# Uneven narrowing, four-unit normalisation rounds, GpSimd scaling and ScalarE first accumulation in an attention and mixture-of-experts kernel

## The chip, the cores and the metric

The kernel runs on one core of one Trainium2 chip. A core has TensorE (PE in the profile; its weight loads are PEld), VectorE (DVE), ScalarE (ACT), GpSimd (POOL) and SyncE (SP, which issues the DMAs here). The metric is the device time of one execution in microseconds, the median of several.

## What is computed

Windowed attention over 4 x 576 tokens is followed by a mixture of eight experts whose weights P come from an iterated (Sinkhorn) normalisation, and that by a two-layer network with a squared ReLU. Cut to the parts that matter here:

```python
logits = x @ w_gate                     # 2304 tokens, 8 experts
P = np.exp(logits - logits.max())
for _ in range(8):
    P /= P.sum(1, keepdims=True) + 1e-09
    P /= P.sum(0, keepdims=True) + 1e-09
    P *= N / E
for e in range(E):                      # FE = 1024 in quarters of 256
    h = np.maximum(x @ w1[e], 0.0)
    out += P[:, e:e + 1] * (h @ w2[e])
h = out @ w_in                          # FF = 2048 in eighths of 256
g = np.maximum(h, 0.0) ** 2
return g @ w_out
```

## The kernel before

**Steps.** After attention, work goes in 80 steps, numbered i = 0 to 79. Steps 0 to 31 take the 32 quarter experts for tokens 0 to 1279 (the first pass, `pair_of(i)` = 0), steps 32 to 63 the same quarters for tokens 1280 to 2303 (the second pass, `pair_of(i)` = 1), and steps 64 to 79 are the two-layer network in the same two passes. A pass treats 1024 tokens by a Strassen-like scheme of seven products; the first pass has 256 tokens more, the "singles".

**Units.** A step is a list of units, each a group of matmuls: u1 to u7 of the first layer (`l1_pair`, six matmuls of 512 columns each), eight units of the second layer of the step before (`l2_units`), and in the first pass four single second-layer units and two single first-layer units of 256 columns. That is 21 units in the first pass and 15 in the second, counted k = 0, 1, ... in the order u1, u2, u3, u4, l2, u5, l2, u6, l2, u7, five l2, then the singles. What is due for other engines is written behind the unit to which it is tied: `after(j, f)` puts `f` behind the unit j places later. All engines run their own instructions in the order in which they are written.

**The banks.** Each l2 unit, each single unit and each small matmul of the normalisation writes one of three PSUM buffers named mm. It comes free when VectorE has added it into the accumulator acc (L647), or, in the first accumulation of a pass, when ScalarE or VectorE has copied it there (L643 for odd column blocks, L645 for even ones). In the first three steps (`i < SCALED`) the hidden values are not scaled by P, since P is not known yet; the accumulator is multiplied by P afterwards, in step 3 (L650).

**Normalisation.** `sinkhorn()` is a generator that is moved on once behind each unit of steps 0 to 2. A round has an opening half on VectorE (five small instructions, L429 to L437, ending in the column sums scs), a matmul on TensorE two units later (L443, sums over partitions), and, a unit after that, a closing half on VectorE (four small instructions, L445 to L448). Before the change the closing half of a round and the opening half of the next stand together, so a round takes three units.

**Narrowing.** The weights of the two-layer network arrive as 64-bit numbers and are turned into float32 in 32 pieces, each in four parts: A starts a load (L165), B is two VectorE instructions on 512 columns (L172, L176), C two (L180, L183), D three and a store (L187, L190, L194, L195). `narrow_on()` does the next part. Before the change it is called behind the units k = 0 and 8 of the steps 3 to 58 (but for 30 to 32), and behind k = 13 of each third step; `settled` completes a piece ahead of step 30, and step 60 begins with all parts that are still missing.

**Other work named below.** `split` of new weights into high and low halves (L129 on ScalarE, L133 on VectorE: w2l, blkl, suml), sums of weight blocks on GpSimd (L142 to L147), the scaling g (L532), its low half gl (L518), the additions into s2 and s3 (L583, L574), and `load_p`, which loads the rows of P for the next expert (L253).

Of the kernel before, what the change touches and what calls it, by code (L numbers as in the profile page):

```python
# [14 lines left out]
ALU = mybir.AluOpType  # L15
# [18 lines left out]
SPE = FE // FB  # L34
# [6 lines left out]
SCALED = 3  # L41
# [5 lines left out]
def tile_kernel(ctx: ExitStack, tc: tile.TileContext, a):  # L47
    nc = tc.nc
    out = a["out"]
# [360 lines left out]
    def sinkhorn():  # L410
        flat = ptile.rearrange("p c e -> p (c e)")
        ones = xb()[:, :128]
        nc.vector.memset(ones, 1.0)
        m1 = sk.tile([128, 1], F32, tag="m1", name="m1")
        m2 = sk.tile([128, 1], F32, tag="m2", name="m2")
        nc.vector.tensor_reduce(out=m1, in_=flat, axis=AX.X, op=ALU.max)
        yield
        ps = bank("mm")
        nc.tensor.transpose(ps[:1, :128], m1, ident)
        nc.vector.tensor_reduce(out=m2[:1], in_=ps[:1, :128], axis=AX.X, op=ALU.max)  # L420
        yield
        ps = bank("mm")
        nc.tensor.matmul(ps[:, :1], ones[:1, :], m2[:1, :], start=True, stop=True)
        nc.vector.tensor_scalar(out=m1, in0=ps[:, :1], scalar1=-1.0, scalar2=None, op0=ALU.mult)
        nc.scalar.activation(out=flat, in_=flat, func=AF.Exp, bias=m1, scale=1.0)
        yield
        for _ in range(8):
            rs = sk.tile([128, NCH, 1], F32, tag="srs", name="srs")
            nc.vector.tensor_reduce(out=rs[:, :, 0], in_=ptile, axis=AX.X, op=ALU.add)  # L429
            nc.vector.tensor_scalar(out=rs, in0=rs, scalar1=1e-9, scalar2=None, op0=ALU.add)  # L430
            nc.vector.reciprocal(out=rs, in_=rs)
            nc.vector.tensor_tensor(
                out=ptile, in0=ptile, in1=rs.to_broadcast([128, NCH, E]), op=ALU.mult
            )
            cs = sk.tile([128, E], F32, tag="scs", name="scs")
            ct = sk.tile([128, 1, E], F32, tag="sct", name="sct")
            nc.vector.tensor_reduce(  # L437
                out=cs, in_=ptile.rearrange("p c e -> p e c"), axis=AX.X, op=ALU.add
            )
            yield  # L440
            yield
            ps = bank("mm")
            nc.tensor.matmul(ps[:, :E], ones, cs, start=True, stop=True)  # L443
            yield
            nc.vector.tensor_scalar(out=ct[:, 0, :], in0=ps[:, :E], scalar1=1e-9, scalar2=None, op0=ALU.add)  # L445
            nc.vector.reciprocal(out=ct, in_=ct)
            nc.vector.tensor_scalar(out=ct, in0=ct, scalar1=float(NTOK) / E, scalar2=None, op0=ALU.mult)
            nc.vector.tensor_tensor(  # L448
                out=ptile, in0=ptile, in1=ct.to_broadcast([128, NCH, E]), op=ALU.mult
            )  # L450
        yield
        for c0, c1 in ((0, 16), (16, NCH)):
            m = (c1 - c0) * E
            ps = bank("mm")
            nc.tensor.transpose(ps[:m, :128], ptile[:, c0:c1, :].rearrange("p c e -> p (c e)"), ident)
            pT = tmp("pT")[:, :128]
            nc.vector.tensor_copy(pT[:m], ps[:m, :128])
            nc.sync.dma_start(p_dram[c0:c1].rearrange("c e n -> (c e) n"), pT[:m])
            yield
        for t in range(2):  # L460
            load_p(0, 0, t)
        load_ps(0)
# [10 lines left out]
    def pair_of(i):  # L473
        return phase(i) % 2
# [16 lines left out]
    def after(k, f):  # L491

        due.setdefault(clock[0] + k, []).append(f)
# [49 lines left out]
    def l1_pair(i):  # L543

        gh = post[0].tile([128, FC, 2 * T], F32R, tag="gh", name="gh", bufs=2)
        gl = post[0].tile([128, FC, 2 * T], F32R, tag="gl", name="gl", bufs=2)
        g_t[i, 0] = gh, gl
        bank_a, bank_b, bank_c = bank("s"), bank("pt"), bank("xt")
        s2, s3 = (post[0].tile([128, 512], F32, tag=n, name=n, bufs=1) for n in ("s2", "s3"))

        def out(fc, t, src, k):
            cols = slice(t * T, t * T + T)
            p = p_t[pair_of(i), steps[i][1] // SPE, t] if steps[i][0] and i >= SCALED else None
            evac_g(i, gh[:, fc, cols], gl[:, fc, cols], src, p, k)

        def u1():
            product(bank_a, i, "blk", 0, 0, start=True)
            after(0, lambda: nc.scalar.copy(bank_b, bank_a))  # L558

        def u2():  # L560
            product(bank_c, i, "sum", 0, 4, start=True)

        def u3():
            product(bank_a, i, "blk", 1, 1, stop=True)
            out(0, 0, bank_a, 0)

        def u4():
            product(bank_b, i, "sum", 1, 5)
            after(0, lambda: nc.scalar.copy(s2, bank_b))  # L569

        def u5():
            product(bank_b, i, "sum", 2, 6)
            after(0, lambda: nc.scalar.copy(s3, bank_b))
            after(1, lambda: nc.vector.tensor_tensor(out=s3, in0=bank_c, in1=s3, op=ALU.add))  # L574
            out(1, 1, s3, 2)

        def u6():
            product(bank_b, i, "blk", 3, 3, stop=True)
            out(1, 0, bank_b, 0 if i < SCALED or not steps[i][0] else 1)

        def u7():
            product(bank_c, i, "sum", 3, 2, stop=True)
            after(0, lambda: nc.vector.tensor_tensor(out=s2, in0=bank_c, in1=s2, op=ALU.add))  # L583
            out(0, 1, s2, 2)
            if steps[i][0] and steps[i][1] % SPE == SPE - 2:
                after(1, lambda: load_p(pair_of(i), steps[i][1] // SPE + 1, 0))
            if steps[i][0] and steps[i][1] % SPE == SPE - 1:
                after(1, lambda: load_p(pair_of(i), steps[i][1] // SPE + 1, 1))

        return [u1, u2, u3, u4, u5, u6, u7]  # L590

    def l1_single(i):
# [21 lines left out]
    def l2_units(i, which):  # L614

        if i < 0 or (i, which) not in g_t:
            return []
        moe, s = steps[i]
        last = s == (NS1 if moe else NS2) - 1
        gh, gl = g_t[i, which]  # L620
        whi, wlo = (z.rearrange("p (f d) -> p f d", f=FC) for z in wset[i % 2]["w2"])
        n = NSG if which else 2 * T
        t0 = SINGLE if which else PAIRS[pair_of(i)]

        def unit(c, h, w):
            ps = bank("mm")
            ps = ps[:, :w] if moe else ps
            k = 0
            for fc in range(FC):
                for g, wt in ((gh, whi), (gl, whi), (gh, wlo)):  # L630
                    if moe:
                        lhsT, rhs = wt[:, fc, c * 128:c * 128 + 128], g[:, fc, h:h + w]
                    else:
                        lhsT, rhs = g[:, fc, c * 128:c * 128 + 128], wt[:, fc]
                    nc.tensor.matmul(ps, lhsT, rhs, start=k == 0, stop=k == 3 * FC - 1)  # L635
                    k += 1
            if moe:
                dst = acc[which].rearrange("p (c n) -> p c n", c=KC)[:, c, h:h + w]
            else:
                dst = acc[which].rearrange("p (c d) -> p c d", d=DM)[:, c]  # L640
            if s == 0:
                if c % 2:
                    nc.scalar.copy(dst, ps)  # L643
                else:
                    nc.vector.tensor_copy(dst, ps)  # L645
            else:
                nc.vector.tensor_tensor(out=dst, in0=ps, in1=dst, op=ALU.add)  # L647
            if i == SCALED - 1:
                p = p_t[0] if which else p_t[0, 0, h // T]
                nc.vector.tensor_tensor(out=dst, in0=dst, in1=p, op=ALU.mult)  # L650
            if last and moe:
                nc.sync.dma_start(y_dram[:, c, t0 + h:t0 + h + w], dst)
            elif last:
                ch = t0 // 128 + c
                nc.sync.dma_start(out[ch * 128:(ch + 1) * 128], dst)

        if moe:
            return [lambda c=c, h=h: unit(c, h, min(T, n)) for h in range(0, n, T) for c in range(KC)]
        return [lambda c=c: unit(c, 0, DM) for c in range(n // 128)]
# [16 lines left out]
    with tc.manual_schedule():  # L676
# [144 lines left out]
        for i in range(len(steps) + 1):  # L821
# [33 lines left out]
            for k, u in enumerate(order):  # L855
                run(u)
                if i < SCALED:
                    next(sink, None)
                if 3 <= i < first[2] - 5 and not slow and (k in (0, 8) or (k == 13 and i % 3 == 0)):
                    narrow_on()  # L860
        settle()

# [77 lines left out]
```

## Time and profile before

| | |
|---|---|
| median of 3 runs | 2089.8 us (2089.55 to 2090.09) |
| the profiled execution, device time | 2094.18 us |
| its span, first to last instruction | 2092.3 us |
| TensorE busy | 2038.7 us, 97% |
| VectorE busy | 1597.5 us, 76% |
| ScalarE, GpSimd busy | 758.0 us, 364.9 us |
| mean granted TensorE clock | 0.995 |

The profile counts a matmul from its start to its modelled end, so neighbours overlap; where TensorE waits it shows as idle time before a matmul. A window over one step gives the length of the step, since each step begins with the first product of u1.

### The profile page before, as it was taken

Reading aid. Unit: us, or ns where it says so; the run is one execution under the profiler, and the core shown is the slowest. Engines: PE = TensorE matmul, PEld = TensorE weight load, DVE = VectorE, ACT = ScalarE, POOL = GpSimd, SP = SyncE. Lnnn points to the kernel's source line nnn. Section 1 sums busy time; section 2 is a strip of 40 time slices with the busy share of each in tenths; the row PEclk is TensorE's granted clock in tenths of the full one; section 3 lists DMA queues with packets and bytes.
Section 4 is the critical chain, followed back from the end, with each engine's and each line's share of the span. In section 5 each row is a group of like instructions: output and inputs, shape, how many; then the busy total and the mean of one; then the engine's idle time right before and its main releaser. Section 6 shows DMA issues by size and latency. Waiting matters only on the chain.

```text
span 2092.3 us, 26392 instructions
## 1 busy us (share of the span) xinstructions
PE 2038.7 (97%) x10230; PEld 1684.7 (81%) x10230; DVE 1597.5 (76%) x2604; ACT 758.0 (36%) x1375; POOL 364.9 (17%) x404
## 2 busy tenths in 40 slices
PE   9989899999999999999999999999999999999999
PEld 7767788888788888888788888888887878887887
DVE  5867777777777777777888888888888786667776
ACT  6752232232232322222343333333333354344542
POOL 2521011111101111111221121212121131113120
PEclk9999999999999999999999999999999999999999
DMA  8622212121212121112322313232323131113111
GB/s 254 192 70 70 63 50 65 47 67 56 66 59 69 58 74 53 52 63 71 125 79 79 86 61 96 66 95 62 96 61 101 61 101 45 38 59 111 61 41 50
DMA packets 67292, 160.63 MB, mean 77 GB/s; under 512 B 6096, under 2 KB 26592, under 8 KB 67168
## 3 DMA queue, kind: packets, MB, share of 16 engines
q1 hardware_dynamic: 67168, 158.96, 24.5%
q8 instruction: 80, 1.31, 0.3%
q14 instruction: 44, 0.36, 0.1%
HBM read 138.94 MB, written 20.00 MB: 76 GB/s over the span
## 4 chain that ended last, share of the span: by engine, by line
PE 83%; DVE 14%; ACT 1%; issue 1%; DMA 1%; SPq 0%; POOL 0%; DVEq 0%; ACTq 0%; POOLq 0%
PE mm L635 39%; PE pt L484 15%; PE s L484 10%; PE xt L484 9%; PE mm L604 5%; DVE acc L647 4%; DVE gl L518 2%; DVE g L532 1%; DVE suml L133 1%; PE mm L735 1%; PE s L296 1%; PE xt L357 1%; PE pt L344 1%; DVE s L583 1%; DVE x_lo L210 1%
## 5 line engine op out<-in xcount | busy, mean ns | idle before, releaser
L647 DVE TENSOR_TENSOR acc<-mm,acc 128x512 f32<-128x512 f32 x746 | 474.6, 643 | 206.1 <-PE mm L635 201.2
L635 PE MATMUL mm<-gl,w2h 128*128 128x512 f32 x1024 | 404.1, 395 | 0.0
L635 PE MATMUL mm<-gh,w2h 128*128 128x512 f32 x1024 | 403.1, 394 | 0.8 <-DVE acc L647 0.7
L635 PE MATMUL mm<-gh,w2l 128*128 128x512 f32 x1024 | 403.7, 394 | 0.0
L540 ACT CAST gh<-g 128x512 fp32r<-128x512 f32 x308 | 191.4, 622 | 581.9 <-DVE g L532 581.6
L142 POOL TENSOR_TENSOR sums<-raw 128x256 f32<-128x256 f32 x80 | 65.5, 819 | 1522.8 <-DVE suml L133 1502.5
L635 PEld LDWEIGHTS mm<-gh,w2h 128*128 128x128 f32 x1024 | 192.9, 188 | 46.5 <-DVE acc L647 2.1
L635 PEld LDWEIGHTS mm<-gl,w2h 128*128 128x128 f32 x1024 | 192.7, 188 | 44.0
L635 PEld LDWEIGHTS mm<-gh,w2l 128*128 128x128 f32 x1024 | 192.8, 188 | 43.5
L518 DVE TENSOR_TENSOR gl<-g,gh 128x512 fp32r<-128x512 f32 x308 | 222.9, 728 | 0.9 <-ACT gh L540 0.9
L532 DVE SCALAR_TENSOR_TENSOR g<-s,pp 128x512 f32<-128x512 f32 x183 | 127.8, 698 | 94.1 <-PE s L484 91.9
L484 PE MATMUL pt<-x_hi,sumh 128*128 128x512 f32 x320 | 127.3, 398 | 4.5 <-ACT s L569 4.5
L484 PE MATMUL s<-x_hi,blkh 128*128 128x512 f32 x320 | 126.4, 395 | 1.0 <-ACT pt L558 1.0
L484 PE MATMUL xt<-x_lo,sumh 128*128 128x512 f32 x320 | 126.1, 394 | 0.0
L484 PE MATMUL pt<-x_lo,sumh 128*128 128x512 f32 x320 | 126.1, 394 | 0.0
L484 PE MATMUL pt<-x_hi,suml 128*128 128x512 f32 x320 | 126.1, 394 | 0.0
L484 PE MATMUL xt<-x_hi,suml 128*128 128x512 f32 x320 | 126.0, 394 | 0.0
L484 PE MATMUL xt<-x_hi,sumh 128*128 128x512 f32 x320 | 125.9, 394 | 0.0
L484 PE MATMUL s<-x_lo,blkh 128*128 128x512 f32 x320 | 125.9, 393 | 0.0
L484 PE MATMUL s<-x_hi,blkl 128*128 128x512 f32 x320 | 125.7, 393 | 0.0
L540 ACT CAST sgh<-g 128x256 fp32r<-128x256 f32 x74 | 29.9, 406 | 244.0 <-DVE g L532 244.0
L133 DVE TENSOR_TENSOR w2l<-raw,w2h 128x1024 fp32r<-128x1024 f32 x80 | 100.6, 1258 | 17.2 <-ACT w2h L129 17.2
(149 smaller groups left out, 4123.5 us busy)
## 6 DMA issues: line engine op xcount, KB each, us to landing
raw<-in_w SPq DMA_DIRECT2D x128, 512.0 KB, 3.5
raw<-w SPq DMA_DIRECT2D x32, 512.0 KB, 3.4
q<-in_q SPq DMA_DIRECT2D x15, 576.0 KB, 5.4
pp<-p_dram SPq DMA_DIRECT2D x32, 256.0 KB, 5.3
xb<-in_w_in SPq DMA_DIRECT2D x16, 512.0 KB, 4.6
w<-xb SPq DMA_DIRECT2D x32, 256.0 KB, 2.1
xb<-in_w_out SPq DMA_DIRECT2D x16, 512.0 KB, 4.6
v<-in_v SPq DMA_DIRECT2D x16, 432.0 KB, 4.6
```

The source lines that it names most:

```text
L133: nc.vector.tensor_tensor(out=w[1], in0=src, in1=w[0].bitcast(F32), op=ALU.subtract)
L142: tt(out=c(sums, 0), in0=c(raw1, 2), in1=c(raw1, 3), op=ALU.add)
L210: return lambda: nc.vector.tensor_tensor(out=x_lo[:, k, j], in0=z, in1=x_hi[:, k, j].bitcast(F32), op=ALU.subtract)
L296: nc.tensor.matmul(ps[:, g, :], qt[:, j, :], kt[:, j * QB:j * QB + KB], start=True, stop=True)
L344: nc.tensor.transpose(ps[:, g * 128:(g + 1) * 128], ex[:, g, :], ident)
L484: nc.tensor.matmul(ps, w[:, c], z[:, x, j], start=start and k == 0, stop=stop and k == 5, skip_group_check=True)
L518: nc.vector.tensor_tensor(out=glo, in0=z, in1=ghi.bitcast(F32), op=ALU.subtract)
L532: nc.vector.scalar_tensor_tensor(out=held["g"], in0=src, scalar=0.0, in1=held["r"], op0=ALU.max, op1=ALU.mult)
L540: after(k + 1, lambda: nc.scalar.copy(ghi, held["g"]))
L604: nc.tensor.matmul(ps, w[:, c], z[:, kc], start=k == 0, stop=k == 3 * KC - 1)
L635: nc.tensor.matmul(ps, lhsT, rhs, start=k == 0, stop=k == 3 * FC - 1)
L647: nc.vector.tensor_tensor(out=dst, in0=ps, in1=dst, op=ALU.add)
```

## The change

Five edits. (1) A `yield` between a closing half and the next opening half makes a round of the normalisation four units long. (2) The load of P's first row block for the next expert goes from u7 of the third quarter to u1 of the fourth quarter of an expert. (3) In step 0's accumulation (done in step 1) all blocks are copied by ScalarE. (4) The multiplication of the accumulator by P in step 3 goes to GpSimd. (5) Narrowing starts at step 5, with two parts a step in the first pass (k = 0, 8) and three in the second (k = 0, 5, 10).

```diff
@@ sinkhorn
             nc.vector.tensor_tensor(
                 out=ptile, in0=ptile, in1=ct.to_broadcast([128, NCH, E]), op=ALU.mult
             )
+            yield
         yield
@@ l1_pair
         def u1():
             product(bank_a, i, "blk", 0, 0, start=True)
+            if steps[i][0] and steps[i][1] % SPE == SPE - 1:
+                after(1, lambda: load_p(pair_of(i), steps[i][1] // SPE + 1, 0))
             after(0, lambda: nc.scalar.copy(bank_b, bank_a))
...
             out(0, 1, s2, 2)
-            if steps[i][0] and steps[i][1] % SPE == SPE - 2:
-                after(1, lambda: load_p(pair_of(i), steps[i][1] // SPE + 1, 0))
@@ l2_units
             if s == 0:
-                if c % 2:
+                if c % 2 or i == 0:
                     nc.scalar.copy(dst, ps)
...
             if i == SCALED - 1:
                 p = p_t[0] if which else p_t[0, 0, h // T]
-                nc.vector.tensor_tensor(out=dst, in0=dst, in1=p, op=ALU.mult)
+                nc.gpsimd.tensor_tensor(out=dst, in0=dst, in1=p, op=ALU.mult)
@@ the loop over steps
-                if 3 <= i < first[2] - 5 and not slow and (k in (0, 8) or (k == 13 and i % 3 == 0)):
+                if SCALED + 2 <= i < first[2] - 5 and not slow and k in ((0, 8), (0, 5, 10))[pair_of(i)]:
                     narrow_on()
```

VectorE in step 1, from the split of the new first-layer weights (blkl) to the end of the next opening half. Before:

```order
L645 COPY acc_1957<-mm 128x512
L133 TENSOR_TENSOR blkl_136<-raw_95,blkh_135 128x1024
L574 TENSOR_TENSOR s_2107<-xt,s_2107 128x512
L445 TENSOR_SCALAR sct<-mm 128x8
L446 RECIPROCAL sct<-sct 128x8
L447 TENSOR_SCALAR sct<-sct 128x8
L448 TENSOR_TENSOR ptile<-ptile,sct 128x144
L429 TENSOR_REDUCE srs<-ptile 128x18
L430 TENSOR_SCALAR srs<-srs 128x18
L431 RECIPROCAL srs<-srs 128x18
L432 TENSOR_TENSOR ptile<-ptile,srs 128x144
L437 TENSOR_REDUCE scs<-ptile 128x8
```

and after, where the closing half stands a unit ahead of the opening half, the s3 addition between them, and no copy into acc is left:

```order
L133 TENSOR_TENSOR blkl_136<-raw_95,blkh_135 128x1024
L445 TENSOR_SCALAR sct<-mm 128x8
L446 RECIPROCAL sct<-sct 128x8
L447 TENSOR_SCALAR sct<-sct 128x8
L448 TENSOR_TENSOR ptile<-ptile,sct 128x144
L577 TENSOR_TENSOR s_2105<-xt,s_2105 128x512
L429 TENSOR_REDUCE srs<-ptile 128x18
L430 TENSOR_SCALAR srs<-srs 128x18
L431 RECIPROCAL srs<-srs 128x18
L432 TENSOR_TENSOR ptile<-ptile,srs 128x144
L437 TENSOR_REDUCE scs<-ptile 128x8
```

In all, VectorE has seven closing and six opening halves in step 1 before, and five of each after; the rest moves into step 2.

GpSimd in steps 2 to 4 after the change, where before only the weight sums (sums) stood:

```order
L147 TENSOR_TENSOR sums<-raw_95,sums 128x256
L651 TENSOR_TENSOR acc_1957<-acc_1957,pp 128x512 x8
L651 TENSOR_TENSOR acc_1958<-acc_1958,ps 128x256 x4
L142 TENSOR_TENSOR sums<-raw_95 128x256
```

The twelve multiplications now stand between the weight sums written in step 3 and those written in step 4.

VectorE in step 35 (second pass), from the weight split to the scaling of s3. Before:

```order
L133 TENSOR_TENSOR blkl_136<-raw_95,blkh_135 128x1024
L647 TENSOR_TENSOR acc_1957<-mm,acc_1957 128x512
L574 TENSOR_TENSOR s_9598<-xt,s_9598 128x512
L532 SCALAR_TENSOR_TENSOR g<-s_9598,pp 128x512
```

and after, with part D at k = 5:

```order
L133 TENSOR_TENSOR blkl_136<-raw_95,blkh_135 128x1024
L187 TENSOR_SCALAR xb<-xb 128x512
L190 SCALAR_TENSOR_TENSOR xb<-xb 128x512
L194 TENSOR_TENSOR xb<-xb 128x512
L648 TENSOR_TENSOR acc_1957<-mm,acc_1957 128x512
L577 TENSOR_TENSOR s_9566<-xt,s_9566 128x512
L533 SCALAR_TENSOR_TENSOR g<-s_9566,pp 128x512
```

Part D now stands ahead of an addition into acc and of the s3 addition, which reads the bank that u7 writes next.

## Rows read from the trace of the kernel before

**Rows 1.** The page: busy time of each engine, and the chain by engine.

```profile
PE 2038.7 (97%) x10230; PEld 1684.7 (81%) x10230; DVE 1597.5 (76%) x2604; ACT 758.0 (36%) x1375; POOL 364.9 (17%) x404
...
PE 83%; DVE 14%; ACT 1%; issue 1%; DMA 1%; SPq 0%; POOL 0%; DVEq 0%; ACTq 0%; POOLq 0%
```

**Rows 2.** Windows: stretch, length, busy us (instructions) by engine, granted clock, DMA share, GB/s.

```profile
149.50:185.50 36.00, 30.82 (x154) 25.19 (x154) 30.05 (x80) 10.35 (x18) 6.78 (x8) 0.95 0.10 30
185.50:212.10 26.60, 26.60 (x142) 22.75 (x140) 15.26 (x24) 7.71 (x12) 3.27 (x4) 1.00 0.37 96
212.10:247.40 35.30, 29.97 (x141) 24.98 (x140) 27.48 (x43) 7.89 (x12) 3.78 (x4) 0.90 0.14 38
247.40:273.90 26.50, 26.50 (x141) 22.65 (x140) 19.94 (x32) 7.90 (x12) 3.33 (x4) 1.00 0.23 75
273.90:963.80 689.90, 672.98 (x3452) 570.87 (x3451) 510.32 (x827) 197.66 (x300) 85.81 (x100) 0.99 0.20 60
329.00:356.50 27.50, 27.09 (x141) 22.79 (x140) 20.60 (x34) 7.91 (x12) 3.30 (x4) 1.00 0.19 58
356.50:383.30 26.80, 26.72 (x141) 22.66 (x139) 18.96 (x31) 7.91 (x12) 3.31 (x4) 1.00 0.22 65
464.10:496.50 32.40, 29.16 (x140) 25.11 (x139) 22.99 (x36) 7.90 (x12) 3.80 (x4) 0.89 0.20 61
...
1044.70:1585.80 541.10, 541.10 (x2341) 439.85 (x2340) 460.41 (x652) 187.54 (x267) 97.28 (x105) 1.00 0.26 80
...
1606.60:1628.60 22.00, 21.12 (x92) 16.88 (x91) 19.82 (x29) 8.05 (x11) 3.20 (x4) 1.00 0.26 84
1628.60:1649.40 20.80, 20.80 (x92) 16.93 (x91) 15.99 (x24) 7.05 (x10) 4.07 (x6) 1.00 0.16 51
```

**Rows 3.** Groups by line: single second-layer matmuls; busy us, mean ns, idle before <-releaser.

```profile
L635 PE MATMUL mm<-sgh,w2h 128*128 128x256 f32 x256 | 77.1, 301 | 23.9 <-DVE acc L647 23.4
```

**Rows 4.** Waits in step 1: us in total, times, longest.

```profile
PE mm L443 <- DVE scs L437: 5.7, 5, 1.9
```

**Rows 5.** Timeline of VectorE, one round of the normalisation (start, duration).

```profile
157.35 0.15 DVE L445 TENSOR_SCALAR sct<-mm 128x8 f32<-128x8 f32 x1
...
159.52 0.42 DVE L437 TENSOR_REDUCE scs<-ptile 128x8 f32<-128x144 f32 x1
```

**Rows 6.** Groups by line: VectorE's copies into the accumulator, step 1.

```profile
L645 DVE COPY acc<-mm 128x512 f32<-128x512 f32 x4 | 2.7, 686 | 1.0 <-PE mm L635 1.0
...
L645 DVE COPY acc<-mm 128x256 f32<-128x256 f32 x2 | 0.8, 420 | 0.7 <-PE mm L635 0.7
```

**Rows 7.** Groups by line: VectorE's multiplications of the accumulator, step 3.

```profile
L650 DVE TENSOR_TENSOR acc<-acc,pp 128x512 f32<-128x512 f32 x8 | 5.6, 695 | 0.3
...
L650 DVE TENSOR_TENSOR acc<-acc,ps 128x256 f32<-128x256 f32 x4 | 1.7, 425 | 0.1
```

**Rows 8.** One line's instructions: GpSimd on 512 columns (ns min/median/max).

```profile
L204 POOL TENSOR_TENSOR xb<-xb x24: 1290/1296/2167, 993.8 to 1909.7; 128x512 f32<-128x512 f32 x24
```

**Rows 9.** Timelines of VectorE and GpSimd in step 3, side by side.

```profile
236.74 1.22 DVE L518 TENSOR_TENSOR gl<-g,gh 128x512 fp32r<-128x512 f32 x1
...
236.23 1.17 POOL L143 TENSOR_TENSOR sums<-raw 128x256 f32<-128x256 f32 x1
```

**Rows 10.** Timeline of step 7, which starts at 329.04: VectorE, and u7 on TensorE.

```profile
337.31 1.22 DVE L133 TENSOR_TENSOR blkl<-raw,blkh 128x1024 fp32r<-128x1024 f32 x1
338.89 0.69 DVE L647 TENSOR_TENSOR acc<-mm,acc 128x512 f32<-128x512 f32 x1 [0.36 <-PE mm L635]
339.50 0.68 DVE L574 TENSOR_TENSOR s<-xt,s 128x512 f32<-128x512 f32 x1
...
341.48 0.39 PE L484 MATMUL xt<-x_hi,sumh 128*128 128x512 f32 x1
...
342.89 0.42 DVE L187 TENSOR_SCALAR xb<-xb 128x512 int32<-128x512 int32 x1
...
344.69 0.68 DVE L518 TENSOR_TENSOR gl<-g,gh 128x512 fp32r<-128x512 f32 x1
```

## The prediction

> **What bounds the kernel now.** I read the page first, then windows cut at the step boundaries, then what ended TensorE's waits inside the steps that are too long, and last the VectorE timelines there. The page says TensorE: 97% busy, 83% of the chain, with VectorE holding 14% of it [rows 1]. So VectorE's 76% is no bound as a mean, and time can only come out of places where TensorE waits for it. The windows show which. The 26 steps 33 to 58 of the second pass take 541.1 us, 20.8 each, with TensorE busy for the whole of it [rows 2]: nothing can be won there, only lost. In the first pass a step without a wait is step 4 with 26.5, but steps 5 to 29 average 689.9 / 25 = 27.6, step 1 takes 36.0 and step 3 35.3 [rows 2]. In three of the long ones the granted clock is 0.95, 0.90 and 0.89, so that part of each ran at the lower of the two levels, 1.2 instead of 2.4 GHz, behind the wait [rows 2]: a long wait costs more than itself. Two waits make up most of it: the single second-layer units wait 23.4 us for VectorE's additions to free a bank [rows 3], and the normalisation's matmul in step 1 waits 5.7 us for the column sums [rows 4].
>
> **Step 1: longer rounds and ScalarE copies.** A round costs VectorE 159.52 + 0.42 - 157.35 = 2.6 us [rows 5]. Before, step 1 holds seven closing and six opening halves, 6.5 rounds or 16.9 us, in 30.05 us of VectorE work [rows 2]; the copies are 2.7 + 0.8 = 3.5 us more [rows 6], the rest about 9.7. After, it holds five rounds (13.0) and no copies: 22.7 us of work for 26.5 us of matmuls. A unit of the second pass is 20.8 / 15 = 1.39 us [rows 2], so a round has 5.5 us instead of 4.2 for its 2.6 and whatever else is queued. TensorE becomes the bound, but an opening half still has only two units, 2.8 us, to reach scs, with splits of 1.22 us [rows 10] queued ahead of it in two rounds; I leave 1.0 us for that and take 27.5. Ends: 26.6 as step 2 [rows 2]; 32 if each of five matmuls still waits the 5.7 / 5 = 1.1 that it did [rows 4]. Gain **8.5** (4 to 9.4). ScalarE gets six copies, some 3.5 us at VectorE's price, on 10.35 of 36 [rows 2]; its idle time covers them. If it ran late, the mm banks would come free late; its load of about half the step doesn't say so.
>
> **Step 2** takes over the 1.5 rounds and the transposes: 3.9 us on VectorE's 15.26, 19.2 in all, less than the 19.94 that step 4 carries without a TensorE wait [rows 2]. Its own small matmuls and one late column sum: loss **0.5** (0 to 1).
>
> **Step 3: scaling on GpSimd.** VectorE loses 5.6 + 1.7 = 7.3 us [rows 7] and the narrowing parts of this step. GpSimd gets eight instructions of 1.30 us [rows 8] and four of half the width, some 13 us, between its weight sums; step 4's additions wait for them a step later, which is cover enough, and the next weight sums are needed only in the second half of step 4. What isn't free is the neighbour: while GpSimd read SBUF (1.17 us for 256 columns), gl, whose two inputs are in SBUF, took 1.22 us instead of the 0.68 of the later one [rows 9, 10], 0.54 more. Eight VectorE instructions of step 3 have both inputs in SBUF (four gl, two g from s2 and s3, two splits) and stand among the multiplications: 8 x 0.54 = 4.3 us. What lateness costs here I take from step 7: its part D adds 344.69 - 342.89 = 1.8 us [rows 10] behind the ninth unit, and the step is 27.5, 1.0 above step 4 [rows 2]. So 4.3 / 1.8 x 1.0 = 2.4 us, step 3 at 28.9, gain **6.4**. Ends: 26.5 without any contention (8.8), and 35.3 as before (0, the second rival).
>
> The Trainium skill (SBUF — State Buffer, Who interferes with whom) says that a VectorE instruction with two SBUF inputs and a GpSimd instruction that reads SBUF exclude each other for the whole instruction. The 1.22 us of gl agree. By that rule the delay is up to a whole 1.30 us each instead of the 0.54 that I scale with.
>
> **Narrowing in the first pass.** From step 5 on two parts a step, so A B and C D take turns. Both occur before: C D in step 7, 27.5, and A B in step 8, 26.8 [rows 2], together 54.3. Steps 5 to 29 become 26.8 + 12 x 54.3 = 678.4 against 689.9: gain **11.5** (9 to 13, the upper end with every A B at 26.7 and D a little cheaper without a third part ahead of it). What goes is the third part of each third step; step 12, with B, C and D, takes 32.4 at clock 0.89 [rows 2].
>
> **Narrowing in the second pass.** Three parts in each of 26 steps instead of in each third. VectorE is at 460.4 / 26 = 17.7 us of 20.8 now [rows 2]; the 17 parts more come to 4.25 pieces of some 4 us (D alone 1.8 [rows 10]), 0.7 us a step: 18.4, or 88%. The 20.8 us of the steps that have three parts now (all within rows 2's 541.1) speak for no loss. The new place k = 5 does cost something: with D there, the s3 addition moves 1.8 us back. In step 7 it ended at 339.50 + 0.68 = 340.18, and u7, which writes the bank it reads, began at 341.48 [rows 10]: 1.3 us of slack, and VectorE idles from 338.5 (the end of blkl) to 338.89, 0.4 us more: about 0.1 to 0.2 short. D falls on k = 5 in six steps: loss **1.2** with something for the rest (0 to 6).
>
> **Step 60** begins with the three missing parts before, 22.0 against 20.8 in step 61 [rows 2]; after, all 128 are done by step 58. Gain **1.2**. Moving load_p by about half a step costs nothing: it still has over ten units, 14 us, and only its place among the loads in SP's queue changes; the wait for its buffer was over an expert ago.
>
> **Sum.** 8.5 - 0.5 + 6.4 + 11.5 - 1.2 + 1.2 = 25.9 us. The profiled execution, 2094.2 (span 2092.3 and 1.9 around it), would come to 2068.3. The median lies 4.4 below that execution; I take the same sum off it: 2089.8 - 25.9 = 2063.9, say **2064**.
>
> **The rivals.**
> - *The rounds are bound by their chain, not by VectorE's load.* Then five rounds at (36.0 - 26.5) / 6.5 = 1.5 us each stay in step 1, the rest moves to step 2, and only the copies (3.5) are won: 8.0 - 3.5 = 4.5 less, 2068.4. For it: scs ends the wait each time [rows 4]. Against: VectorE is at 83% in that step and rounds of 2.6 us fit twice into four units.
> - *GpSimd takes back what it relieves.* If each of the eight instructions waits a whole multiplication, 8 x 1.30 = 10.4 us exceed the 7.3 removed, step 3 stays at 35.3 with its clock fall, and the sum is 6.4 smaller: 2070.3. For it: rows 9. Against: a GpSimd instruction also waits for VectorE, and the first three multiplications are two units apart.
>   The Trainium skill (Perfetto Trace Analysis, Optimizing Scalar/DVE Operations) warns of exactly this, that moving work between these two might not help; rows 9 bear out the contention, not yet its size here.
> - *The second pass runs out of VectorE (slower).* First-pass steps with a third part cost (689.9 - 17 x 27.15) / 8 = 28.5, 1.4 more than those with two. If each of the 26 second-pass steps paid 1.4, that is 36 us: 2064 + 36 - 1.2 = 2099. It decides from 25.9 / 26, or 1.0 us a step on top. For it: 88% load, no singles to wait but a burst of five additions in a row. Against: rows 2, 541.1 us without any wait, three-part steps included.
> - *The change does little*, if lateness only wanders into the following steps and the clock falls there: 2064 + 20 = 2084. Against: step 4 recovered fully behind step 3 [rows 2].
>
> **How the numbers follow.** Forecast (all terms near their values) 0.62, chain rival 0.13, GpSimd rival 0.15, both faster as well; second pass 0.05, slower; little 0.05, at 2084 on the edge, so 0.02 faster and 0.03 the same. The best ends together give 9.4 + 8.8 + 13 + 1.2 = 32.4, 2057.4; the chain rival and the GpSimd rival together 10.9 more than 2064, 2074.9. Eight in ten: **2056.5 to 2074**. A measurement here can tell about 0.2%, 4 us, from no change: faster 0.92, within 0.2% 0.03, slower 0.05.
>
> **What would show it.** In the profile after: step 1 below 29 us with TensorE's waits for scs under 2 us and clock 1.00; step 3 at 27 to 31, with gl and the splits over 1 us beside GpSimd's multiplications; steps 5 to 29 alternating near 27.5 and 26.8, with no window under clock 0.99; second-pass steps at 20.8 with some tenths more in each fourth; step 60 at 20.8. The forecast is wrong if second-pass windows exceed 21.5 on average, if the clock falls in step 3, or if a first-pass step with only A B or C D passes 28.

## The result and the profile after

The changed kernel takes 2065.4 us in the median of four runs (2063.2 to 2067.1) against 2090.0 (2089.55 to 2093.8): a ratio of 0.9878, 95% interval 0.9861 to 0.9895, 24.6 us less. The forecast was 2064.0 in a range of 2056.5 to 2074.0. The profiled execution took 2067.1 us, its span 2065.3.

The page of the changed kernel, busy times and the chain by engine, beside [rows 1]:

```profile
PE 2029.6 (98%) x10230; PEld 1673.7 (81%) x10230; DVE 1575.6 (76%) x2586; ACT 761.3 (37%) x1381; POOL 376.8 (18%) x416
...
PE 87%; DVE 11%; ACT 1%; DMA 1%; issue 0%; SPq 0%; POOL 0%; DVEq 0%; ACTq 0%; POOLq 0%
```

VectorE is as busy as before in the mean. What fell is its share of the chain, from 14% to 11%. The windows of the changed kernel, with columns as in [rows 2] (stretch, length, busy us by engine, granted clock, DMA), are steps 0, 1, 2, 3, then 5 to 29 in one, 6, 7, 31, 33 to 58 in one, 35, and 60:

```profile
132.20:147.90 15.70, 14.15 (x73) 10.95 (x72) 9.05 (x24) 6.91 (x12) 0.00 (x0) 1.00 0.35 114
147.90:176.20 28.30, 28.25 (x152) 23.81 (x150) 24.14 (x62) 14.36 (x26) 6.79 (x8) 1.00 0.11 38
176.20:203.30 27.10, 27.10 (x146) 23.06 (x145) 18.38 (x38) 7.71 (x12) 3.27 (x4) 1.00 0.31 76
203.30:231.30 28.00, 26.95 (x140) 22.63 (x139) 20.76 (x27) 7.89 (x12) 15.37 (x12) 1.00 0.16 47
...
257.90:935.50 677.60, 671.01 (x3452) 566.82 (x3451) 493.67 (x811) 197.69 (x300) 82.92 (x100) 1.00 0.20 59
284.60:312.10 27.50, 26.95 (x140) 22.67 (x139) 20.59 (x34) 7.91 (x12) 3.31 (x4) 1.00 0.26 77
312.10:338.80 26.70, 26.70 (x140) 22.64 (x139) 18.96 (x31) 7.90 (x12) 3.32 (x4) 1.00 0.15 50
962.00:1006.30 44.30, 42.60 (x212) 36.01 (x211) 37.90 (x57) 15.93 (x27) 14.36 (x12) 0.96 0.33 104
1018.00:1560.00 542.00, 542.00 (x2342) 438.78 (x2341) 470.49 (x680) 187.68 (x267) 98.31 (x105) 1.00 0.27 85
1059.60:1080.60 21.00, 21.00 (x92) 16.82 (x90) 18.91 (x29) 7.07 (x10) 4.60 (x5) 1.00 0.33 101
1580.80:1601.60 20.80, 20.80 (x92) 16.91 (x91) 15.15 (x22) 8.03 (x11) 2.60 (x4) 1.00 0.16 51
```

Beside [rows 2]: step 1 goes from 36.0 to 28.3 (28.4 from matmul to matmul; a window is cut at tenths) with TensorE busy all but 0.05 us of it by the modelled ends of its matmuls, step 3 from 35.3 to 28.0 with the clock at 1.00 instead of 0.90, steps 5 to 29 from 689.9 to 677.6, step 60 from 22.0 to 20.8. The second pass pays 0.9 us. And the single second-layer matmuls, which waited 23.4 us for VectorE's additions [rows 3], wait 9.2 (the same view, by line):

```profile
L636 PE MATMUL mm<-sgh,w2h 128*128 128x256 f32 x256 | 76.7, 300 | 9.3 <-DVE acc L648 9.2
```

By step (lengths from windows at the step boundaries, in us; the minus sign is a gain):

| place | forecast | measured in the two profiled executions |
|---|---|---|
| attention, before step 0 | 0 | -0.8 |
| step 0 | 0 | -0.9 |
| step 1 | -8.5 | -7.7 |
| step 2 | +0.5 | +0.5 |
| step 3 | -6.4 | -7.2 |
| steps 5 to 29 | -11.5 | -12.3 |
| step 31 | 0 | +1.6 |
| steps 33 to 58 | +1.2 | +0.9 |
| step 60 | -1.2 | -1.2 |
| all | -25.9 | -27.1 |

The medians differ by 24.6 and not 27.1 us because the profiled execution of before lies 4.2 us above its median and that of after 1.7. The three large terms of the forecast each miss by 0.8 us, step 1 short and the other two over. The three places without a term (-0.8, -0.9 and +1.6) add up to -0.1 us; that they cancel is luck.

### The profile page after: what moved, and what is told of

Same layout as the page of the kernel before. It is cut to its first block, busy times and chain, and to the rows that moved or that the text cites. A ratio compares the mean times of both kernels' runs of the same rounds, so it can differ in the third digit from the quotient of the medians.

```text
span 2065.3 us, 26402 instructions
## 1 busy us (share of the span) xinstructions
PE 2029.6 (98%) x10230; PEld 1673.7 (81%) x10230; DVE 1575.6 (76%) x2586; ACT 761.3 (37%) x1381; POOL 376.8 (18%) x416
## 4 chain that ended last, share of the span: by engine, by line
PE 87%; DVE 11%; ACT 1%; DMA 1%; issue 0%; SPq 0%; POOL 0%; DVEq 0%; ACTq 0%; POOLq 0%
PE mm L636 42%; PE pt L485 16%; PE s L485 10%; PE xt L485 9%; PE mm L605 6%; DVE acc L648 3%; DVE gl L519 2%; DVE g L533 1%; PE mm L736 1%; PE s L296 1%; DVE suml L133 1%; PE xt L357 1%; PE pt L344 1%; DVE x_lo L210 1%; DVE s L586 0%
```

## The experiments

Each is the changed kernel with one edit, but for the first, which is the kernel before with one. Where only one execution was timed, the lengths of the steps in its trace are what is compared; they repeat within 0.1 us from kernel to kernel in nearly all steps where nothing was changed, so a step says more than the total, which is 2 us up or down by the attention part and the clock alone.

**The new sharing out of the narrowing alone**, on the kernel before:

```diff
-                if 3 <= i < first[2] - 5 and not slow and (k in (0, 8) or (k == 13 and i % 3 == 0)):
+                if SCALED + 2 <= i < first[2] - 5 and not slow and k in ((0, 8), (0, 5, 10))[pair_of(i)]:
```

> The kernel before with the new sharing out of the narrowing alone. Additive theory: steps 5 to 29 at 677.6 us (690.0 before), 33 to 58 at 542.0 (541.1), step 60 at 20.8 (21.9), and step 3, without its parts, 2 to 4 us shorter than 35.3; together 14.5 to 17 us, 2073 to 2075.5. Rival: the edits only work together, since late work of steps 1 to 3 wanders on; then steps 5 to 29 stay above 683 and the total above 2080.

2076.2 us (2075.0 to 2077.7), ratio 0.9936 (0.9919 to 0.9952), 13.2 less than before. Its windows of step 1, step 3, steps 5 to 29, step 31 and steps 33 to 58:

```profile
147.10:181.70 34.60, 29.49 (x153) 23.98 (x153) 29.96 (x80) 10.42 (x18) 6.76 (x8) 1.00 0.10 31
...
208.30:239.80 31.50, 28.71 (x140) 24.20 (x139) 24.54 (x39) 7.88 (x12) 4.24 (x4) 0.95 0.15 42
266.30:943.90 677.60, 671.04 (x3452) 567.21 (x3451) 493.59 (x811) 197.65 (x300) 82.79 (x100) 1.00 0.20 59
...
970.40:1014.70 44.30, 42.60 (x213) 36.02 (x212) 37.94 (x57) 15.91 (x27) 14.35 (x12) 0.96 0.31 104
1026.30:1568.50 542.20, 542.20 (x2342) 439.03 (x2341) 470.63 (x680) 187.69 (x267) 98.15 (x105) 1.00 0.27 85
```

Steps 5 to 29 are at 677.6 with or without the other edits, so this one adds up by itself, and step 3 gains 3.8 us of its 7.2 without its narrowing parts, the clock there at 0.95 instead of 0.90. The total is 0.7 us above the 2073 to 2075.5 that were expected. In the profiled execution step 31 is 1.6 us longer than before, at clock 0.96; whether it was in the other three is not known. Step 1 shows something that the two main profiles hide: its program is that of before, and it took 34.6 us at clock 1.00 instead of 36.0 at 0.95. So 1.4 us of its 7.7 us gain are the clock's.

**Rounds of three units again:**

```diff
                 out=ptile, in0=ptile, in1=ct.to_broadcast([128, NCH, E]), op=ALU.mult
             )
-            yield
         yield
```

> The changed kernel with rounds of three units again, ScalarE keeping all first copies. Load theory: VectorE has 26.6 us of work in step 1, so step 1 is 29 to 31 us against 28.4 and TensorE waits for scs 1 to 2.5 us. Chain rival: the wait is the length of the chain through scs and not the load; step 1 stays near 36.0 - 3.5 = 32.5 or above, with waits for scs of 4 us or more.

2069.5 us. Step 1 is 32.6 us, and the load theory, which gave 29 to 31 and waits for scs of 1 to 2.5 us, fails. Its window, and the waits for scs and for the banks in it (us in total, times, longest):

```profile
148.10:180.70 32.60, 29.11 (x155) 23.97 (x154) 26.85 (x74) 13.33 (x23) 6.78 (x8) 1.00 0.09 34
```

```profile
PE mm L443 <- DVE scs L437: 2.9, 3, 1.9
...
PE mm L443 <- ACT acc L643: 1.2, 2, 0.6
```

VectorE's work is what I had worked out, 26.85 us against 26.6, but it fills only 82% of the step: TensorE waits while VectorE has time over. The longest wait, 1.9 us, is the first of the step, ahead of any copy. The chain rival had the length, 32.5, but not the waits: it asked for 4 us or more, and they are 2.9.

**Half of the first copies back on VectorE**, rounds of four units:

```diff
-                if c % 2 or i == 0:
+                if c % 2:
                     nc.scalar.copy(dst, ps)
```

> The changed kernel with half of the first copies back on VectorE, rounds of four units. Load theory: 3.5 us more on VectorE (27.6 us in all) fit under the 28.4 us of step 1 in the mean, so step 1 is 28.4 to 30 us. Chain rival: the copies stand in the chain and their 3.5 us come back in full, 31.9 us.

2065.7 us, step 1 at the upper end of the load theory's range and below the chain rival's 31.9:

```profile
146.50:176.50 30.00, 28.68 (x152) 23.85 (x151) 26.89 (x68) 11.28 (x20) 6.88 (x8) 1.00 0.12 36
```

VectorE has the same 26.9 us as with rounds of three units, and the step is 2.6 us shorter. That is what the longer round is worth at the same load; the lower load of the changed kernel, 24.1 us, is worth the other 1.6. With the undisturbed 34.6 of step 1 the two edits add up to within 0.4 us: the copies give 34.6 - 32.6 = 2.0, and four units on top of them 32.6 - 28.4 = 4.2; the other way about 34.6 - 30.0 = 4.6 and 30.0 - 28.4 = 1.6. The chain rival's 32.5 for the three-unit kernel came true by chance: it started from 36.0, of which 1.4 was the clock's.

**The added unit ahead of the matmul instead of ahead of the opening half**, to see what about four units helps:

```diff
             )
             yield
             yield
+            yield
             ps = bank("mm")
...
                 out=ptile, in0=ptile, in1=ct.to_broadcast([128, NCH, E]), op=ALU.mult
             )
-            yield
         yield
```

> Rounds of four units with the added unit ahead of the matmul instead of ahead of the opening half: closing and opening half stand together again, and scs has three units instead of two. Deadline theory: what counts is that scs is there when TensorE comes to the matmul; step 1 is 28.0 to 29.0 us (28.4 in the changed kernel) with no wait for scs over 0.3 us. Load-spreading theory: the nine instructions in one piece of 2.6 us hold up the other work as before; step 1 is 30 us or more.

2066.5 us. Step 1 and, below it, step 2:

```profile
147.30:175.50 28.20, 27.97 (x150) 23.68 (x149) 24.07 (x62) 14.32 (x26) 6.87 (x8) 1.00 0.12 38
175.50:202.70 27.20, 27.20 (x147) 23.11 (x146) 18.35 (x38) 7.70 (x12) 3.26 (x4) 1.00 0.28 76
```

No wait for scs is left. So it isn't the spreading of VectorE's nine instructions that helps; three units from a closing half to the next matmul, instead of two, do it in either form. Steps 1 and 2 together take 55.3 us in this form and 55.4 in the changed kernel. VectorE's work in step 1 is the same in the two, 24.1 us, and 2.7 us higher in the three-unit kernel, so this run alone doesn't part the later matmul from the lower load; the run before it, with 26.9 us, does.

**The multiplication by P left out:**

```diff
-            if i == SCALED - 1:
-                p = p_t[0] if which else p_t[0, 0, h // T]
-                nc.gpsimd.tensor_tensor(out=dst, in0=dst, in1=p, op=ALU.mult)
```

> The changed kernel without the multiplication of the accumulator by P (left out altogether, so the first three quarter experts are unscaled). Contention theory: what is left of step 3 above 26.5 us (28.1 in the changed kernel) comes from GpSimd's multiplications holding up VectorE instructions with two SBUF inputs; step 3 falls to 26.5 to 26.8 and gl is back at 0.68 us. Rival: VectorE's own additions and splits make the wait; step 3 stays at 27.5 to 28.1.

**The multiplication back on VectorE:**

```diff
-                nc.gpsimd.tensor_tensor(out=dst, in0=dst, in1=p, op=ALU.mult)
+                nc.vector.tensor_tensor(out=dst, in0=dst, in1=p, op=ALU.mult)
```

> The changed kernel with the multiplication by P back on VectorE, narrowing still starting at step 5. Load theory: 7.3 us more on VectorE at the 1.0 us per 1.8 us that part D costs in step 7 give step 3 30.6 us (29.5 to 32), more if the clock falls behind the wait. Rival (GpSimd takes back what it relieves): no worse than the changed kernel's 28.1, at most 28.5. Second rival: the narrowing parts were not what made step 3 long, so it stays at 33 to 35.

**Half of it back on VectorE:**

```diff
-                nc.gpsimd.tensor_tensor(out=dst, in0=dst, in1=p, op=ALU.mult)
+                tt = nc.vector.tensor_tensor if c % 2 else nc.gpsimd.tensor_tensor
+                tt(out=dst, in0=dst, in1=p, op=ALU.mult)
```

> The changed kernel with the multiplication by P of the odd column blocks back on VectorE, of the even ones on GpSimd. Lateness theory: VectorE gets 3.6 us of its own and is held up half as much (about 2.0 instead of the 3.9 us that its instructions with two SBUF inputs take longer in step 3 of the changed kernel), 5.6 in all, and step 3 goes from 28.1 to 28.5 to 29.0. Rival: GpSimd's unbroken run of eight is what hurts, so that breaking it up brings step 3 to 27.5 or less.

The totals were 2061.5, 2070.1 and 2065.5 us. Step 3 of the three, in this order, is 26.5 us and 31.2, both as the theory had them, and 29.3, 0.3 more than the 28.5 to 29.0 expected; none of the rivals held:

```profile
200.80:227.30 26.50, 26.50 (x141) 22.59 (x139) 17.53 (x27) 7.88 (x12) 3.33 (x4) 1.00 0.17 50
```

```profile
204.40:235.60 31.20, 28.39 (x141) 24.08 (x140) 24.55 (x39) 7.89 (x12) 4.25 (x4) 0.95 0.13 43
```

```profile
202.40:231.70 29.30, 27.55 (x140) 22.72 (x139) 23.41 (x33) 7.89 (x12) 9.24 (x8) 1.00 0.15 45
```

With the changed kernel's 28.0 this is a ladder by VectorE's busy time: 17.5 us without the multiplications give 26.5, 20.8 with them on GpSimd 28.0, 23.4 with half of them 29.3, 24.6 with all on VectorE 31.2, the last with the clock at 0.95. Up to the 29.3 each us more of VectorE's work comes with about 0.5 us more of the step. Without the multiplications the two splits are back at 1.22 us and gl at 0.72 in the mean. In the changed kernel the timelines of VectorE and, below, of GpSimd in step 3 (start, duration) show where VectorE's 3.2 us more come from:

```profile
211.54 2.32 DVE L133 TENSOR_TENSOR blkl<-raw,blkh 128x1024 fp32r<-128x1024 f32 x1
...
215.09 1.29 DVE L533 SCALAR_TENSOR_TENSOR g<-s,pp 128x512 f32<-128x512 f32 x1
216.31 0.68 DVE L648 TENSOR_TENSOR acc<-mm,acc 128x512 f32<-128x512 f32 x1
216.91 0.67 DVE L533 SCALAR_TENSOR_TENSOR g<-pt,pp 128x512 f32<-128x512 f32 x1
217.51 1.40 DVE L519 TENSOR_TENSOR gl<-g,gh 128x512 fp32r<-128x512 f32 x1
```

```profile
211.11 1.67 POOL L651 TENSOR_TENSOR acc<-acc,pp 128x512 f32<-128x512 f32 x1 [10.81 <-DVE acc L648]
214.54 1.29 POOL L651 TENSOR_TENSOR acc<-acc,pp 128x512 f32<-128x512 f32 x1 [1.77 <-DVE acc L648]
217.06 1.30 POOL L651 TENSOR_TENSOR acc<-acc,pp 128x512 f32<-128x512 f32 x1 [1.23 <-DVE acc L648]
```

The split blkl ends 1.08 us after the first multiplication (211.11 + 1.67 = 212.78, and 213.86), about as long as it takes alone. gl ends 0.55 after the third (218.36, and 218.91). g from pt, with one input in PSUM, keeps its 0.67 us though most of it runs beside the third, and the eight additions of 512 columns into acc keep 0.68 in the mean. The Trainium skill (SBUF — State Buffer, Who interferes with whom) states that an instruction of VectorE with two SBUF inputs contends with one of GpSimd that reads SBUF, and that what they share is locked exclusively. The runs agree.

**The second pass's middle part at k = 6 instead of 5:**

```diff
-                if SCALED + 2 <= i < first[2] - 5 and not slow and k in ((0, 8), (0, 5, 10))[pair_of(i)]:
+                if SCALED + 2 <= i < first[2] - 5 and not slow and k in ((0, 8), (0, 6, 10))[pair_of(i)]:
```

> The changed kernel with the second pass's middle part at k = 6, behind the s3 addition, instead of k = 5. Theory: in each fourth step of the second pass (35, 39 and so on, 21.0 us) part D ahead of the s3 addition holds up u7; these steps return to 20.8 and steps 33 to 58 to 540.9 to 541.1, 1 us less. Rival: VectorE's load of about 88% makes the 0.2 us; then 542 stays.

2064.1 us (2063.0 to 2065.3), which can't be told from the changed kernel by the total. The steps tell it: 33 to 58 in one window, a little below the 540.9 to 541.1 expected, and step 35.

```profile
1017.80:1558.50 540.70, 540.70 (x2341) 439.58 (x2340) 467.59 (x680) 187.62 (x267) 98.31 (x105) 1.00 0.27 85
1059.40:1080.20 20.80, 20.80 (x92) 16.92 (x91) 18.62 (x29) 7.05 (x10) 4.60 (x6) 1.00 0.32 101
```

Part D ahead of the s3 addition was the cause. In step 35 of the changed kernel that addition on VectorE ends at 1071.37 + 0.68 = 1072.05, and u7 on TensorE starts at 1072.11:

```profile
1071.37 0.68 DVE L577 TENSOR_TENSOR s<-xt,s 128x512 f32<-128x512 f32 x1
```

```profile
1072.11 0.50 PE L485 MATMUL xt<-x_hi,sumh 128*128 128x512 f32 x1
```

**The same in both passes:**

```diff
-                if SCALED + 2 <= i < first[2] - 5 and not slow and k in ((0, 8), (0, 5, 10))[pair_of(i)]:
+                if SCALED + 2 <= i < first[2] - 5 and not slow and k in ((0, 6), (0, 6, 10))[pair_of(i)]:
```

> The same, and the first pass's second part at k = 6 instead of k = 8. Place theory: D two units earlier is worked off before the run of five second-layer units, so C D steps fall from 27.5 to 26.6 to 27.0 and A B steps from 26.7 to 26.5; steps 5 to 29 from 677.6 to 663 to 670, the total to 2050 to 2058. Load rival: VectorE's sum over a step is the same, so steps 5 to 29 stay at 675 or more. Slower rival: D at k = 6 delays the scaling of s3 and the bank of u6, and steps reach 28.

2049.0 us (2047.7 to 2049.8), ratio to the kernel before 0.9804 (0.9790 to 0.9819): faster than both kernels, and 1 us below the range that was expected. Its steps 5 to 29 in one window, step 6 (parts C and D), step 7 (A and B), and step 31:

```profile
255.70:919.20 663.50, 663.50 (x3452) 566.16 (x3451) 494.17 (x811) 197.62 (x300) 83.13 (x100) 1.00 0.20 60
282.30:308.80 26.50, 26.50 (x140) 22.62 (x139) 20.44 (x34) 7.90 (x12) 3.32 (x4) 1.00 0.26 80
308.80:335.40 26.60, 26.60 (x141) 22.69 (x140) 19.15 (x31) 7.90 (x12) 3.32 (x4) 1.00 0.16 50
945.70:988.40 42.70, 40.99 (x212) 34.43 (x211) 37.97 (x57) 16.03 (x27) 15.12 (x12) 1.00 0.32 108
```

VectorE does the same work in step 6 as in the changed kernel (20.44 against 20.59 us), but TensorE no longer waits. Over the whole kernel the single second-layer matmuls wait 2.7 us instead of 9.2:

```profile
L636 PE MATMUL mm<-sgh,w2h 128*128 128x256 f32 x256 | 73.9, 289 | 2.7 <-DVE acc L648 2.7
```

The load is not what cost 1.0 us in each C D step; two units later was too late.

**The load of P at its old place:**

```diff
         def u1():
             product(bank_a, i, "blk", 0, 0, start=True)
-            if steps[i][0] and steps[i][1] % SPE == SPE - 1:
-                after(1, lambda: load_p(pair_of(i), steps[i][1] // SPE + 1, 0))
...
             out(0, 1, s2, 2)
+            if steps[i][0] and steps[i][1] % SPE == SPE - 2:
+                after(1, lambda: load_p(pair_of(i), steps[i][1] // SPE + 1, 0))
```

> The changed kernel with the load of P's first block at its old place (u7 of the third quarter). Theory: the move is worth nothing; no step differs by more than 0.05 us but for step 31, which is 42.8 or 44.3 us by the granted clock whatever the kernel. Rival: the old place sits among other loads and holds one up; then steps 3, 7, 11 and so on differ.

2066.6 us, and no step differs from the changed kernel's by more than 0.05 us. Steps 5 to 29 and 33 to 58:

```profile
257.40:935.00 677.60, 671.00 (x3452) 566.85 (x3451) 493.71 (x811) 197.68 (x300) 82.77 (x100) 1.00 0.20 59
...
1017.50:1559.50 542.00, 542.00 (x2341) 438.85 (x2340) 470.53 (x680) 187.68 (x267) 98.34 (x105) 1.00 0.27 85
```

## Why the prediction was right, step by step

**The narrowing in the first pass** was the surest term, since both kinds of step stood in the trace of before. Forecast -11.5, measured -12.3: an A B step takes 26.70 where I had taken the 26.8 of one that followed a C D step of the old pattern. The price was right, but the reading beside it, that VectorE's lateness in general makes it, was too loose. The run with k = 6 shows it to be a matter of place: 663.5 us with the same work.

**Step 3** came out at 28.0 to 28.1 (forecast 28.9). The contention is shown by the three multiplication runs. Its size, 8 x 0.54 = 4.3 us of longer instructions, was near the 20.76 - 17.53 = 3.2 us by which VectorE is busier; the price of such lateness, 1.0 us for 1.8, was somewhat high: 1.55 us for 3.2. The GpSimd rival falls. It counted a whole multiplication of 1.30 us for each of eight instructions; two of the four gl met none, and the longest wait of TensorE in step 3 was 0.7 us, where it had been 3.5 before with the clock at 0.90.

**Step 1** is where the reasoning failed although the term held (27.5 forecast, 28.4 measured). Of the 7.7 us gained 1.4 are luck, the clock's; the edits are worth 6.3 (34.6 to 28.4) of the forecast 8.5. I compared VectorE's work with the step's length and left 1.0 us for late column sums. The runs show that the deadline weighs more: with three units from the closing half to the matmul and 24.1 us of VectorE work no wait for scs remains, however the instructions are grouped, while the three-unit kernel waits 2.9 us for scs at a VectorE load of 82%. The load counts as well: with 26.9 us of work the four-unit kernel takes 1.6 us longer and waits 1.2 us for scs. I had put that work at 22.7. In the changed kernel no matmul of the normalisation waits for scs:

```profile
L443 PE MATMUL mm<-scs,xb 128*128 128x8 f32 x16 | 2.3, 218 | 0.0
```

So the 1.0 us was wrong, and so was the floor of 26.6 that I took from step 2. Step 2 of before holds none of these matmuls. Step 1 of the changed kernel holds six, each of two instructions, and is 1.9 us above 26.5. What one of them costs stands in the timeline of TensorE:

```profile
160.86 0.39 PE L636 MATMUL mm<-gh,w2l 128*128 128x512 f32 x1
161.09 0.28 PE L443 MATMUL mm<-scs,xb 128*128 128x8 f32 x2
161.23 0.48 PE L485 MATMUL xt<-x_hi,sumh 128*128 128x512 f32 x1
161.55 0.40 PE L485 MATMUL xt<-x_lo,sumh 128*128 128x512 f32 x1
```

From 161.09 to 161.55 are 0.46 us, where one product alone takes the 0.23 from 160.86 to 161.09. So each costs 0.23 us and the six 1.4. Short waits of the weight loads in this step are the likely rest; the modelled ends of the matmuls cover them:

```profile
PEld xt L485 <- DVE suml L133: 0.5, 1, 0.5
...
PEld mm L443 <- issue: 0.2, 1, 0.2
```

Step 2's +0.5 us came out as forecast, but not for the reason given in part: no late column sum is in it, only small matmuls. The gain in step 0 (0.9 us) was not in the sum: with rounds of four units one matmul leaves that step, and the three-unit kernel has the 16.6 us of before again.

**The second pass** paid by the mechanism named, part D ahead of the s3 addition: 0.2 us in each of the six steps where it falls, 1.2 as forecast, and nothing with k = 6. The net is 0.9 because the kernel before was not free of waits there, as the prediction took it to be. Its steps 46 and 58 took 21.04 us from matmul to matmul, 0.25 more than the others; the window of step 46, cut at tenths:

```profile
1315.00:1336.10 21.10, 21.10 (x92) 16.88 (x91) 18.98 (x28) 7.00 (x10) 4.10 (x5) 1.00 0.32 99
```

The slower rival falls too: with 470.5 us of VectorE work in 542.0 us, 87%, only those six steps lose anything to speak of.

**What had no term** is step 31, 1.6 us longer. Inside the step the program differs in nothing but one load, and the kernel with that load at its old place has the 44.3 us too. Its cause is the granted clock, below.

## What to carry to other kernels

A work item that may be done at any time should stand where the queue behind it has slack, and that is read from what waits next, not from the engine's load alone: the same part D costs 1.0 us behind the ninth unit of a first-pass step and nothing two units earlier. When a short matmul waits for a chain on another engine, moving the matmul later can be worth as much as thinning out that engine's work: here 2.6 us against 1.6. Before work goes to GpSimd, count VectorE's instructions with two SBUF inputs beside it; here moving 7.3 us cost 3.2 us of VectorE time back and still paid (step 3 went from 31.2 to 28.0).

## What the runs showed of the hardware

The same wait is answered by the clock in one execution and not in the next. In step 31 TensorE waits 1.36 us in the kernel before and 1.37 in the changed one for the same addition (timelines of TensorE, one row of each):

```profile
1013.70 0.39 PE L635 MATMUL mm<-sgh,w2h 128*128 128x256 f32 x1 [1.36 <-DVE acc L647]
```

```profile
985.43 0.38 PE L636 MATMUL mm<-sgh,w2h 128*128 128x256 f32 x1 [1.37 <-DVE acc L648]
```

but the windows of 9 us around it have a granted clock of 1.00 before and 0.81 after (the first is of the kernel before):

```profile
1011.00:1020.00 9.00, 7.32 (x54) 6.52 (x53) 8.98 (x15) 2.98 (x6) 3.39 (x3) 1.00 0.28 87
```

```profile
982.70:991.70 9.00, 7.30 (x44) 6.61 (x43) 8.81 (x14) 2.87 (x5) 3.35 (x3) 0.81 0.28 93
```

In the second, part of the stretch ran at 1.2 instead of 2.4 GHz. Of the twelve profiled kernels here seven have step 31 at 42.7 to 42.8 us and five at 44.3, with nothing between. No single edit divides the five from the seven, but each kernel was profiled once, and what decides between the two was not tried. As far as these runs tell it is 1.6 us of luck in each profile, as the 1.4 us in step 1 of before were, and a reason to compare steps and not totals where an edit is worth a microsecond.
